# One padded transpose, one joint normalisation and a new order in a three-stage attention and mixture kernel

## The chip, the cores and the metric

The kernel runs on one core of a Trainium2 chip. The metric is the device time of one execution, in microseconds (us). The engines are named as in the profile: PE (matrix products, with PEld for loading the stationary operand), DVE, ACT and POOL (elementwise work), SP (starts the transfers).

## The reference

Three stages follow each other on 4 batches of 448 rows:

```python
scores = (q @ k.T) / 8, masked causally         # 4 batches x 12 heads, 448 x 448, head size 64
attn = exp(scores - max) / sum                  # row by row
x = attn @ v                                    # -> 448 x 768 for each batch
h = relu(x @ w_in)                              # 768 -> 1024
gate = sigmoid(conv over 3 neighbouring rows of h)
x = (h * gate) @ w_out                          # 1024 -> 768
logits = x @ w_gate; the best 2 of 4 experts, softmaxed      # per row
for each expert: q, k, v = x @ wq, wk, wv; out += weight * (causal attention(q, k, v) @ wo)
```

All inputs are float32 in value, the result is 4 x 448 x 768.

## The kernel before, in words

**Attention.** Heads are taken in pairs: 24 pairs in the first stage (6 for each batch) and 8 pairs of experts in the last. `scores` (L625) makes the scores of one pair. The rows of a head lie in four chunks of 64, 128, 128 and 128 rows (c = 0 to 3); chunk c is as wide as the causal mask leaves it, 64, 192, 320 or 448 columns, so a head has four score tiles in two PSUM banks. The first pair of all is computed from the plain inputs (L667). All others are split into a high and a low part, and the products of both heads (three terms for each tile) go to PE as one block of 24 instructions (L676), head 0 in the upper 64 rows of the array and head 1 in the lower 64. DVE then adds the mask and takes the row minimum (L653), ACT takes the exponential with its row sum (L657). For each head DVE adds the row sum and the epsilon (L692) and inverts (L694). After that each of the four chunks of the head is scaled by its reciprocal (L698 on ACT, L701 on DVE or POOL; the experts' coefficient is multiplied in here). The chunks of both heads lie side by side in one tile `e`, 2048 columns wide; the columns from 1920 on hold chunk 0 of both heads, in the upper 64 rows alone.

**Weighing.** `weigh` (L712) turns the scaled weights, 128 x 128 at a time, on PE (L710, through the helper `tr`), 16 turns for a pair. The turn of chunk 0 takes both heads at once: 64 rows with 128 columns become 128 rows with 64 columns, so it uses half of the array's rows; the other 15 take 128 rows. Each four turns fill one PSUM bank, which ACT or DVE copies to SBUF. Then follow the products with v: one over the diagonal chunk (L729, two instructions in the profile) and twelve on half of the array's columns (L735).

**The folded weights.** `w_out` and the experts' projections are multiplied once, at the start, into one matrix (`fold`, L843), from high and low parts (L883), while the first pairs' attention runs.

**The rest.** `products` (L875) issues the three-term products of the hidden layer, the projections and the output, at L883.

**Order.** No loop order reaches the engines as written. Every step is a node with the engines that may take it, an assumed cost for each, and what it reads and writes; a planner (`Plan`, L171) plays the engines through in time and picks the ready node of highest rank. The ranks are then shifted by a list of numbers, `SHIFTS`, over ranges of nodes or of time. All turns have the same assumed cost there, `TURN`, whatever their rows. A dependency within one engine needs no wait; between engines it is a semaphore.

**Filling.** Ten products on zeros (L588) come first on PE, and 30 more (L1085) are placed where the planner finds room.

Of the kernel before, what the change touches and what calls it, by code (L numbers as in the profile page):

```python
# [9 lines left out]
F32 = mybir.dt.float32  # L10
# [3 lines left out]
OP = mybir.AluOpType  # L14
# [21 lines left out]

COL2 = (1920, 1536, 896, 0)
# [5 lines left out]
TURNS = ((0, 4), (4, 6))  # L43
# [7 lines left out]
QUOTA = {"xs": 7, "qks": 4, "y": 4, "vs": 3, "vs2": 2, "w1": 3, "wraw": 1, "ab": 4}  # L51
# [478 lines left out]
def attention_moe_moe(ctx: ExitStack, tc: tile.TileContext, qk, vv, w_in, cw, w_out, wqk, wvg, wo, out):  # L530
# [26 lines left out]
    def tiles(name, n, shape, dtype, pool=None):  # L557
        return [(pool or base).tile(shape, dtype, name=f"{name}{i}") for i in range(n)]

    stats = tiles("stat", 4, [128, 4, 4], F32)  # L560
# [13 lines left out]

    bk = Kind(blocks)
# [13 lines left out]
    for name, kind, quota in (  # L589
            ("xs", pairs, QUOTA["xs"]), ("g", pairs, 8), ("qks", pairs, QUOTA["qks"]), ("wx", pairs, 12),  # L590
            ("y", pairs, QUOTA["y"]), ("q2", pairs, 2), ("k2", pairs, 2),
            ("vs", bk, QUOTA["vs"]), ("gx", gxk, 1), ("vs2", bk, QUOTA["vs2"]), ("w1", slabs, QUOTA["w1"]), ("wraw", half, QUOTA["wraw"]), ("wt", half, 2), ("wxr", half, 2), ("raw", half, 1),
            ("xc", half, 2), ("cv", half, 3), ("o", half, 3), ("gw", half, 1),
            ("hp", Kind(hps), 2), ("st", Kind(stats), 4),
            ("e", Kind(tiles("e", EN, [128, 2048], F32)), EN), ("kb", half, 1), ("ab", half, QUOTA["ab"]),
            ("qw", half, 1),
            ("sx", bank, 2), ("sy", bank, 2),
            ("ta", bank, 1), ("t1", bank, 2), ("tb", bank, 2),
            ("po", bank, PO), ("pf", sums, 2), ("fill", sums, 1)):
        P.tag(name, kind, quota)  # L600
# [21 lines left out]
    NORM = {}  # L622


    def scores(qk, j, e):  # L625
# [8 lines left out]
        sts = [P.buf("st") for _ in range(2)]  # L634
# [12 lines left out]
        def weight(o, c):  # L647

            w, st, sb, rows = Q0[c] + QN[c], sts[o], sbs[o], slice(0, QN[c])

            def mx(_):
                m = mask[rows, 448 - w:448] if c and o else mask[rows, 320:320 + w]
                nc.vector.tensor_tensor_reduce(out=ec(o, c), in0=bank(o, c), in1=m, scale=-0.125, scalar=3.0e38,  # L653
                                               op0=OP.add, op1=OP.min, accum_out=st[rows, 0, c:c + 1])

            def ex(_):
                nc.scalar.activation(ec(o, c), ec(o, c), AF.Exp, bias=st[rows, 0, c:c + 1], scale=-1.0,  # L657
                                     accum_out=st[rows, 1, c:c + 1])

            P.op({"V": on_vector(w)}, mx, r=[(sb[c], c)], w=[(e, (o, c)), (st, ("m", c))])  # L660
            P.op({"A": on_scalar(w) + 0.23}, ex, r=[(st, ("m", c))], w=[(e, (o, c)), (st, ("s", c))])
# [22 lines left out]
        for o, st in enumerate(sts):  # L684
            norms(j + o, st, o, ec, e)

    def norms(j, st, o, ec, e):
        moe = j >= B * H
        b, x = divmod(j - B * H, E)


        P.op({"V": 0.09}, lambda _: nc.vector.tensor_reduce(st[:, 3], st[:, 1:3].rearrange("p a c -> p c a"), axis=AX.X, op=OP.add),  # L692
             r=[(st, ("s", c)) for c in range(4)], w=[(st, "r")])
        P.op({"V": 0.095}, lambda _: nc.vector.reciprocal(st[:, 3], st[:, 3]), w=[(st, "r")])  # L694
        for c in ORDER:
            def norm(en, c=c):
                if en == "A":
                    nc.scalar.activation(ec(o, c), ec(o, c), AF.Copy, scale=st[:QN[c], 3, c:c + 1])  # L698
                else:
                    gate = coef[:QN[c], b, c, x:x + 1] if moe else 1.0  # L700
                    engine(en).tensor_scalar(ec(o, c), ec(o, c), st[:QN[c], 3, c:c + 1], gate, op0=OP.mult, op1=OP.mult)  # L701

            cost = scale_cost(Q0[c] + QN[c])
            if moe:
                cost.pop("A", None)
# [436 lines left out]
```

## Time and profile before

| | us |
|---|---|
| median of 3 runs | 545.47 (545.29 to 546.98) |
| the profiled execution: its own time | 546.95 |
| its span, first to last instruction | 545.2 |
| PE busy | 538.5 (99% of the span) |
| DVE, ACT, POOL busy | 410.1 (75%), 335.2 (61%), 114.7 (21%) |

The engines run beside each other, so the busy times do not add up. A product's row gives the duration of one instruction with its fill and drain (270 ns for a turn), which overlaps with its neighbours; what one costs in a row of them is the distance from its start to the next one's start.

### The profile page before, as it was taken

The page shows a single profiled execution, that of the slowest core. Times are in us where ns is not written, and L with a number is a line of the kernel's source. Part 1 is how long each engine was busy: PE and PEld are TensorE (multiplying, and loading weights), DVE is VectorE, ACT ScalarE, POOL GpSimd, SP SyncE. Part 2 cuts the span into 40 slices and gives each one's busy share as a digit, 9 for nine tenths or more (in the row PEclk, how much of TensorE's full clock was granted, in tenths as well). Part 3 has the DMA queues.
Part 4 walks back from the last instruction along what each step waited for, and adds up shares of the span by engine and source line. Part 5 has one row for each costly group of instructions (what it writes and reads, how often), then busy time and mean ns, then how long its engine had stood idle before and what let it go on. Part 6 is the DMA issues. An engine that isn't in the chain of part 4 may idle for free.

```text
span 545.2 us, 10297 instructions
## 1 busy us (share of the span) xinstructions
PE 538.5 (99%) x3552; PEld 439.6 (81%) x3552; DVE 410.1 (75%) x1273; ACT 335.2 (61%) x951; POOL 114.7 (21%) x132
## 2 busy tenths in 40 slices
PE   8899999999999999999999999999999999999999
PEld 4578896778777897899887777998897778988976
DVE  4997788999998464986477999982368999852761
ACT  2673447779997462763475876873268766641742
POOL 4531013629433020020051332300002102000000
PEclk9899999999999999999999999999999999999999
DMA  8884334666664100546012462670004404620042
GB/s 253 247 217 118 117 135 125 229 198 225 210 228 141 33 3 17 181 167 225 1 52 71 125 199 70 222 253 17 1 35 137 149 4 173 203 87 1 2 159 103
DMA packets 43413, 69.92 MB, mean 128 GB/s; under 512 B 8928, under 2 KB 37344, under 8 KB 43360
## 3 DMA queue, kind: packets, MB, share of 16 engines
q1 hardware_dynamic: 43360, 69.26, 39.4%
q8 instruction: 28, 0.46, 0.3%
q14 instruction: 25, 0.20, 0.1%
HBM read 55.87 MB, written 13.37 MB: 127 GB/s over the span
## 4 chain that ended last, share of the span: by engine, by line
PE 90%; DVE 7%; DMA 2%; issue 1%; ACT 0%; SPq 0%; DVEq 0%; ACTq 0%
PE pf L883 52%; PE bank L710 13%; PE bank L676 9%; PE bank L735 8%; PE bank L729 4%; PE pf L990 1%; DVE work L912 1%; DVE pair L617 1%; DMA work<-in_qk 1%; PE bank L883 1%; DMA work<-in_w_out 1%; DVE e L653 1%; DVE work L804 1%; DVE work L806 1%; PE pf L1085 1%
## 5 line engine op out<-in xcount | busy, mean ns | idle before, releaser
L883 PE MATMUL pf<-pair,slab 128*128 128x448 f32 (+2 forms) x984 | 215.6, 366 | 2.9 <-POOL pair L617 1.2
L883 PEld LDWEIGHTS pf<-pair,slab 128*128 128x128 f32 x984 | 172.2, 189 | 24.1 <-issue 4.6
L657 ACT ACTIVATE e<-e,stat 128x320 f32<-128x320 f32 (+3 forms) x256 | 127.0, 498 | 32.7 <-DVE stat L653 32.1
L653 DVE CUSTOM_DVE_ANT_0 e<-bank,mask 64x64 f32<-64x64 f32 (+3 forms) x256 | 92.5, 413 | 15.0 <-PE bank L676 12.8
L710 PE MATMUL bank<-ident,e 128*128 128x128 f32 (+1 forms) x512 | 84.1, 282 | 0.8 <-ACT hp L901 0.4
L710 PEld LDWEIGHTS bank<-ident,e 128*128 128x128 f32 (+1 forms) x512 | 61.7, 142 | 27.6 <-issue 15.5
L883 PE MATMUL pf<-pair,wqks 128*128 128x448 f32 x384 | 81.8, 369 | 0.0
L883 PEld LDWEIGHTS pf<-pair,wqks 128*128 128x128 f32 x384 | 71.3, 188 | 6.0 <-issue 0.6
L617 POOL TENSOR_TENSOR pair<-work,pair 128x448 fp32r<-128x448 f32 (+1 forms) x36 | 44.6, 1254 | 52.3 <-DVE pair L611 26.3
L611 DVE COPY work<-bank 128x512 f32<-128x512 f32 (+1 forms) x64 | 41.9, 670 | 15.7 <-PE bank L710 13.9
L609 ACT ACTIVATE work<-bank 128x512 f32<-128x512 f32 (+1 forms) x68 | 38.3, 576 | 24.9 <-PE bank L710 21.7
L676 PE MATMUL bank<-pair,pair 64*64 64x64 f32 (+3 forms) x560 | 51.9, 293 | 0.0
L698 ACT ACTIVATE e<-e,stat 128x320 f32<-128x320 f32 (+3 forms) x96 | 42.6, 498 | 11.7 <-DVE stat L694 11.1
L735 PE MATMUL bank<-work,block 128*64 128x128 f32 (+2 forms) x384 | 48.5, 388 | 0.0
L657 ACT ACTIVATION_READ_ACCUMULATOR e<-e,stat 128x1 f32 (+1 forms) x256 | 48.2, 188 | 0.0
L912 DVE SCALAR_TENSOR_TENSOR work<-hp,cws,work 128x448 f32<-128x448 f32 x64 | 44.7, 713 | 2.9 <-ACT work L907 2.3
L617 DVE TENSOR_TENSOR pair<-pf,pair 128x448 fp32r<-128x448 f32 (+3 forms) x32 | 15.4, 501 | 39.6 <-ACT pair L609 39.4
L676 PEld LDWEIGHTS bank<-pair,pair 64*128 64x128 f32 (+1 forms) x560 | 40.0, 173 | 3.4 <-issue 1.5
L613 POOL TENSOR_SCALAR pair<-work 128x896 fp32r<-128x896 f32 (+2 forms) x16 | 17.6, 1101 | 103.8 <-DMA block<-in_vv 57.8
L735 PEld LDWEIGHTS bank<-work,block 128*64 128x64 f32 x384 | 22.5, 136 | 20.7 <-issue 19.2
L883 PE MATMUL pf<-wvs,pair 128*128 128x260 f32 x288 | 37.4, 287 | 0.0
L609 ACT ACTIVATE pair<-pf 128x448 fp32r<-128x448 f32 (+3 forms) x32 | 13.3, 444 | 38.7 <-PE pf L883 37.5
(97 smaller groups left out, 628.0 us busy)
## 6 DMA issues: line engine op xcount, KB each, us to landing
slab<-w_scratch SPq DMA_DIRECT2D x24, 768.0 KB, 4.3
work<-in_w_out SPq DMA_DIRECT2D x8, 768.0 KB, 5.1
work<-in_w_in SPq DMA_DIRECT2D x8, 768.0 KB, 5.7
w_scratch<-slab SPq DMA_DIRECT2D x8, 768.0 KB, 4.4
work<-in_qk SPq DMA_DIRECT2D x24, 224.0 KB, 4.4
out<-work SPq DMA_DIRECT2D x24, 224.0 KB, 2.0
block<-in_vv SPq DMA_DIRECT2D x24, 192.0 KB, 3.3
slab<-wo_scratch SPq DMA_DIRECT2D x6, 768.0 KB, 4.6
```

The lines of the kernel that those rows point to most:

```text
L609: nc.scalar.activation(dst(), src(), AF.Copy)
L611: nc.vector.tensor_copy(dst(), src())
L617: return lambda e: engine(e).tensor_sub(dst(), src(), f32(h()))
L653: nc.vector.tensor_tensor_reduce(out=ec(o, c), in0=bank(o, c), in1=m, scale=-0.125, scalar=3.0e38, op0=OP.add, op1=OP.min, accum_out=st[ro ...
L657: nc.scalar.activation(ec(o, c), ec(o, c), AF.Exp, bias=st[rows, 0, c:c + 1], scale=-1.0, accum_out=st[rows, 1, c:c + 1])
L676: nc.tensor.matmul(bank(o, c), q(s)[own, Q0[c]:Q0[c] + QN[c]], k(t)[own, kc(o, c)], start=i == 0, stop=i == 2)
L698: nc.scalar.activation(ec(o, c), ec(o, c), AF.Copy, scale=st[:QN[c], 3, c:c + 1])
L710: P.op({"T": TURN}, lambda _: nc.tensor.transpose(dst()[:, :n], src()[:n], ident[:n, :n]), r=r, w=keys)
L729: P.op({"T": 4 * S / 2400}, lambda _: nc.tensor.matmul(ps[:, :S], v[:, 0].rearrange("p o d -> p (o d)"), n0[:, :S], start=True, stop=False ...
L735: nc.tensor.matmul(ps[own, Q0[k]:S], v[:, k, o], part(o), start=False, stop=k == 2)
L883: nc.tensor.matmul(out_ap(), a(), b(), start=first, stop=end), r=r, w=[(ps, 0)])
L912: return lambda _: nc.vector.scalar_tensor_tensor(cv[:, :S], hp[:, i:S + i], cws[:, fc, i:i + 1], cv[:, :S], op0=OP.mult, op1=OP.add)
```

## The change

- The turn of chunk 0 takes all 128 rows of `e`. The lower 64 rows of its columns are set to zero once, at the start, by POOL, for each of the three `e` tiles. Its result is 128 columns wide, of which the second 64 fall on the place that chunk 1's turn writes afterwards in the same bank; the extra key `(t, max(c, 1))` makes chunk 1 come after it.
- The row sums of both heads lie in one `stat` tile of twice the size, and one reduction and one reciprocal serve both heads; the scaling of either head waits for them. There are 3 such tiles where there were 4 single ones.
- The scaling steps are listed chunk by chunk with both heads inside, not head by head.
- `SHIFTS` is another list, of 48 entries where there were 64, and the order is planned anew. The quotas and costs of the other steps are the same.

```diff
 SHIFTS = (
-    (22128, 169, 174, 0.25), (15400, 176, 216, 0.5), (27611, 179, 259, 0.5), (50220, 85, 105, 0.5),
...
+    (-1, 2486, 2507, -0.5), (57162, 82, 87, 10), (62964, 276, 356, 1), (63391, 321, 331, 2), (-1, 2573, 2593, -32),
...
-    stats = tiles("stat", 4, [128, 4, 4], F32)
+    stats = tiles("stat", 3, [128, 4, 2, 4], F32)
...
+    weights = tiles("e", EN, [128, 2048], F32)
+    for t in weights:
+        nc.gpsimd.memset(t[HALF[1], COL2[0]:], 0.0)
...
-        P.op({"V": 0.09}, lambda _: nc.vector.tensor_reduce(st[:, 3], st[:, 1:3].rearrange("p a c -> p c a"), axis=AX.X, op=OP.add),
-             r=[(st, ("s", c)) for c in range(4)], w=[(st, "r")])
-        P.op({"V": 0.095}, lambda _: nc.vector.reciprocal(st[:, 3], st[:, 3]), w=[(st, "r")])
+        P.op({"V": 0.1}, lambda _: nc.vector.tensor_reduce(st[:, 3].rearrange("p o c -> p (o c)"), st[:, 1:3].rearrange("p a o c -> p (o c) a"), axis=AX.X, op=OP.add),
+             r=[(st, ("s", o, c)) for o in range(2) for c in range(4)], w=[(st, "r")])
+        P.op({"V": 0.11}, lambda _: nc.vector.reciprocal(st[:, 3], st[:, 3]), w=[(st, "r")])
         for c in ORDER:
-            def norm(en, c=c):
...
+            for o in range(2):
+                def norm(en, c=c, o=o):
...
-    def tr(dst, src, r, keys, n=128):
+    def tr(dst, src, r, keys):
 
-        P.op({"T": TURN}, lambda _: nc.tensor.transpose(dst()[:, :n], src()[:n], ident[:n, :n]), r=r, w=keys)
+        P.op({"T": TURN}, lambda _: nc.tensor.transpose(dst(), src(), ident[:, :]), r=r, w=keys)
...
-               [(e, (o, c)) for o in range(2)], [(t, c)], QN[c])
+               [(e, (o, c)) for o in range(2)], [(t, c), (t, max(c, 1))])
```

PE, in the hidden layer of the second batch, before: L883 are its products, L710 the turns (the row with 128x64 is chunk 0's), `e` the weights of a pair.

```order
1131 L883 MATMUL pf_141<-pair_134,slab_137 128x448
1132 L883 MATMUL pf_142<-pair_120,slab_137 128x448
1133 L883 MATMUL pf_142<-pair_120,slab_138 128x448
1134 L710 MATMUL bank_145<-ident,e_159 128x64
1135 L710 MATMUL bank_145<-ident,e_159 128x128 x3
1136 L710 MATMUL bank_144<-ident,e_159 128x128 x2
1137 L883 MATMUL pf_142<-pair_120,slab_137 128x448
```

The same engine and layer in the change, where the lines have the numbers L877, L704 and, for the products on half of the columns, L729:

```order
1093 L729 MATMUL bank_151<-work_143,block_97 64x128 x2
1094 L729 MATMUL bank_151<-work_143,block_97 64x256 x2
1095 L704 MATMUL bank_146<-ident,e_113 128x128 x4
1096 L877 MATMUL pf_145<-pair_126,slab_140 128x448
1097 L877 MATMUL pf_145<-pair_126,slab_141 128x448
1098 L704 MATMUL bank_150<-ident,e_113 128x128 x4
1099 L877 MATMUL pf_145<-pair_126,slab_140 128x448
```

The single row of 128x64 is gone; chunk 0 is one of the four turns of full size.

DVE, at the end of a pair's exponentials in the first stage, before: L692 is the reduction, L694 the reciprocal, L701 a scaling, `stat` one head's sums.

```order
238 L617 TENSOR_TENSOR pair_121<-bank_145,pair_121 128x448
239 L692 TENSOR_REDUCE stat_84<-stat_84 128x4
240 L694 RECIPROCAL stat_84<-stat_84 128x4
241 L701 TENSOR_SCALAR e_161<-e_161,stat_84 128x320
242 L701 TENSOR_SCALAR e_161<-e_161,stat_84 128x448
243 L692 TENSOR_REDUCE stat_85<-stat_85 128x4
244 L694 RECIPROCAL stat_85<-stat_85 128x4
```

DVE at such a place in the change (L685, L687, L695; L608 are copies):

```order
226 L608 COPY work_143<-bank_151 128x512
227 L614 TENSOR_TENSOR wvs<-pf_145,wvs 128x260
228 L685 TENSOR_REDUCE stat_84<-stat_84 128x8
229 L687 RECIPROCAL stat_84<-stat_84 128x8
230 L695 TENSOR_SCALAR e_115<-e_115,stat_84 128x320
231 L695 TENSOR_SCALAR e_115<-e_115,stat_84 64x64
```

Two reductions and two reciprocals became one of each, and all scalings of the pair stand behind them.

PE after the first filling products, before: L883 with 512 or 260 columns are the folded weights, L667 the scores of the first pair.

```order
56 L883 MATMUL pf_141<-pair_120,slab_137 128x512
57 L883 MATMUL pf_142<-pair_120,slab_137 128x260
58 L667 MATMUL bank_145<-work_140 64x64
59 L667 MATMUL bank_146<-work_140 128x320
60 L667 MATMUL bank_146<-work_140 128x192
61 L883 MATMUL pf_141<-pair_120,slab_137 128x512
62 L883 MATMUL pf_141<-pair_121,slab_137 128x512
63 L667 MATMUL bank_145<-work_140 128x448
```

The same place in the change (L661 are the first pair's scores, L1079 filling products, L877 the folded weights):

```order
53 L661 MATMUL bank_151<-work_143 128x192
54 L661 MATMUL bank_148<-work_143 128x192
55 L661 MATMUL bank_149<-work_143 64x64
...
60 L661 MATMUL bank_150<-work_143 64x64
...
65 L877 MATMUL pf_144<-pair_121,slab_140 128x512
66 L877 MATMUL pf_145<-pair_121,slab_140 128x260
67 L877 MATMUL pf_144<-pair_121,slab_140 128x512
68 L877 MATMUL pf_144<-pair_122,slab_140 128x512
```

All eight score products of the first pair now stand ahead of the first folded product, and the second pair's scores follow its first ten.

## Rows read from the trace of the kernel before

**Rows 1.** Page, part 1: busy us (share of span) and instructions by engine.
```profile
PE 538.5 (99%) x3552; PEld 439.6 (81%) x3552; DVE 410.1 (75%) x1273; ACT 335.2 (61%) x951; POOL 114.7 (21%) x132
```
**Rows 2.** Windows: stretch, its us, each engine's busy us, PEclk, DMA share, GB/s.
```profile
17.50:23.50 6.00, 3.67 (x19) 2.38 (x17) 5.93 (x15) 4.27 (x13) 4.62 (x5) 1.00 0.81 254
23.50:27.00 3.50, 3.29 (x14) 2.72 (x14) 2.41 (x5) 2.11 (x5) 1.17 (x1) 0.55 0.99 278
40.00:200.00 160.00, 158.82 (x1089) 130.23 (x1088) 136.44 (x392) 112.49 (x319) 56.16 (x49) 1.00 0.47 152
200.00:400.00 200.00, 200.00 (x1333) 168.59 (x1333) 144.41 (x458) 118.31 (x338) 29.23 (x36) 1.00 0.33 109
400.00:537.00 137.00, 137.00 (x922) 112.25 (x921) 97.43 (x333) 78.81 (x232) 11.47 (x15) 1.00 0.28 95
```
**Rows 3.** Waits of PE: line, for whom, total us, times, longest.
```profile
PE pf L588 <- DVE tri L549: 1.7, 1, 1.7
PE pf L883 <- POOL pair L617: 1.2, 1, 1.2
PE pf L883 <- DVE pair L617: 1.0, 1, 1.0
PE pf L883 <- ACT hp L901: 0.7, 1, 0.7
PE bank L710 <- ACT hp L901: 0.4, 1, 0.4
PE bank L710 <- ACT e L698: 0.2, 1, 0.2
```
**Rows 4.** Timeline of PE near 212 us: start us, us to the last one's end, instructions.
```profile
212.09 0.49 PE L710 MATMUL bank<-ident,e 128*128 128x128 f32 x3
```
**Rows 5.** Timeline of PE, 211 to 217 us: turns of chunk 0 between others.
```profile
211.30 0.39 PE L735 MATMUL bank<-work,block 128*64 128x256 f32 x2
211.62 0.27 PE L710 MATMUL bank<-ident,e 64*128 64x64 f32 x1
211.82 0.44 PE L710 MATMUL bank<-ident,e 128*128 128x128 f32 x2
...
215.70 0.49 PE L710 MATMUL bank<-ident,e 128*128 128x128 f32 x3
216.12 0.27 PE L710 MATMUL bank<-ident,e 64*128 64x64 f32 x1
216.32 0.54 PE L735 MATMUL bank<-work,block 128*64 128x384 f32 x1
```
**Rows 6.** Groups by shape: line, engine, tile of the array, count, busy us, mean ns, idle before.
```profile
L710 PE MATMUL bank<-ident,e 128*128 128x128 f32 x480 | 78.7, 282 | 0.8 <-ACT hp L901 0.4 <-ACT e L698 0.2
L710 PE MATMUL bank<-ident,e 64*128 64x64 f32 x32 | 8.8, 275 | 0.0
L710 PEld LDWEIGHTS bank<-ident,e 64*128 64x128 f32 x32 | 4.4, 137 | 6.8 <-issue 5.4 <-DVE stat L653 0.9
```
**Rows 7.** Timeline of PE, 17 to 24 us.
```profile
17.99 0.49 PE L710 MATMUL bank<-ident,work 128*128 128x128 f32 x3
19.67 1.32 PE L883 MATMUL pf<-pair,slab 128*128 128x512 f32 x6 [1.19 <-POOL pair L617]
20.82 1.15 PE L710 MATMUL bank<-ident,e 128*128 128x128 f32 x4
23.00 0.62 PE L883 MATMUL pf<-pair,slab 128*128 128x512 f32 x2 [1.02 <-DVE pair L617]
```
**Rows 8.** Groups by shape on DVE, ACT and POOL that the change touches.
```profile
L694 DVE RECIPROCAL stat<-stat 128x4 f32<-128x4 f32 x64 | 10.4, 171 | 1.1
L692 DVE TENSOR_REDUCE stat<-stat 128x4 f32<-128x8 f32 x64 | 9.3, 151 | 2.6 <-ACT e L657 2.4
L657 ACT ACTIVATE e<-e,stat 128x192 f32<-128x192 f32 x64 | 28.4, 445 | 11.5 <-DVE stat L653 11.4
L657 ACT ACTIVATION_READ_ACCUMULATOR e<-e,stat 128x1 f32 x192 | 36.1, 188 | 0.0
```
**Rows 9.** Timeline of POOL, 3 to 12 us.
```profile
2.99 1.24 POOL L572 MEMSET block<- 64x64 f32 x7
4.17 0.97 POOL L771 MEMSET work<- 64x448 f32 x2
10.57 1.83 POOL L617 TENSOR_TENSOR pair<-work,pair 128x772 fp32r<-128x772 f32 x1 [5.43 <-ACT pair L609]
```
**Rows 10.** Timeline of PE, first folded product and first scores.
```profile
10.49 0.62 PE L883 MATMUL pf<-pair,slab 128*128 128x512 f32 x2
11.04 1.23 PE L667 MATMUL bank<-work 128*64 128x64 f32 x5
```
**Rows 11.** Timeline of DVE: reductions of the two heads of two pairs.
```profile
400.49 0.15 DVE L692 TENSOR_REDUCE stat<-stat 128x4 f32<-128x8 f32 x1
400.76 0.15 DVE L692 TENSOR_REDUCE stat<-stat 128x4 f32<-128x8 f32 x1
...
421.51 0.15 DVE L692 TENSOR_REDUCE stat<-stat 128x4 f32<-128x8 f32 x1
424.18 0.15 DVE L692 TENSOR_REDUCE stat<-stat 128x4 f32<-128x8 f32 x1
```

More of the change, by code (lines that the diff above doesn't have):

```diff
@@ L34 @@
 HALF = (slice(0, 64), slice(64, 128))
+TURNS = ((0, 4), (4, 6))
 COL2 = (1920, 1536, 896, 0)
@@ L42 @@
 TILES = (((0, 1, 1), (0, 2, 1), (0, 3, 1), (0, 3, 3)), ((1, 1, 1), (1, 2, 1), (1, 3, 1), (1, 3, 3)), ((0, 2, 2), (0, 3, 2), (1, 2, 2), (1, 3, 2)))
-TURNS = ((0, 4), (4, 6))
 SWITCH = 0.2
@@ L50 @@
 PAIRS, VALUES, UNITS, SLABS, EN, PO = 18, 6, 15, 3, 3, 1
-QUOTA = {"xs": 7, "qks": 4, "y": 4, "vs": 3, "vs2": 2, "w1": 3, "wraw": 1, "ab": 4}
+QUOTA = {"xs": 7, "qks": 4, "y": 4, "vs": 3, "vs2": 2, "w1": 3, "wraw": 1, "ab": 4, "qw": 1, "kb": 1, "raw": 1}
 WARM = 10
@@ L591, in attention_moe_moe @@
             ("y", pairs, QUOTA["y"]), ("q2", pairs, 2), ("k2", pairs, 2),
-            ("vs", bk, QUOTA["vs"]), ("gx", gxk, 1), ("vs2", bk, QUOTA["vs2"]), ("w1", slabs, QUOTA["w1"]), ("wraw", half, QUOTA["wraw"]), ("wt", half, 2), ("wxr", half, 2), ("raw", half, 1),
+            ("vs", bk, QUOTA["vs"]), ("gx", gxk, 1), ("vs2", bk, QUOTA["vs2"]), ("w1", slabs, QUOTA["w1"]), ("wraw", half, QUOTA["wraw"]), ("wt", half, 2), ("wxr", half, 2), ("raw", half, QUOTA["raw"]),
             ("xc", half, 2), ("cv", half, 3), ("o", half, 3), ("gw", half, 1),
-            ("hp", Kind(hps), 2), ("st", Kind(stats), 4),
-            ("e", Kind(tiles("e", EN, [128, 2048], F32)), EN), ("kb", half, 1), ("ab", half, QUOTA["ab"]),
-            ("qw", half, 1),
+            ("hp", Kind(hps), 2), ("st", Kind(stats), 3),
+            ("e", Kind(weights), EN), ("kb", half, QUOTA["kb"]), ("ab", half, QUOTA["ab"]),
+            ("qw", half, QUOTA["qw"]),
             ("sx", bank, 2), ("sy", bank, 2),
@@ L620, in load @@
         return lambda e: nc.sync.dma_start(dst(), src)
-    NORM = {}
     def scores(qk, j, e):
@@ L633, in scores @@
             sb[0], sb[1] = sb[3], sb[2]
-        sts = [P.buf("st") for _ in range(2)]
+        st = P.buf("st")
         def bank(o, c):
@@ L647, in weight @@
         def weight(o, c):
-            w, st, sb, rows = Q0[c] + QN[c], sts[o], sbs[o], slice(0, QN[c])
+            w, sb, rows = Q0[c] + QN[c], sbs[o], slice(0, QN[c])
             def mx(_):
@@ L653, in mx @@
                 nc.vector.tensor_tensor_reduce(out=ec(o, c), in0=bank(o, c), in1=m, scale=-0.125, scalar=3.0e38,
-                                               op0=OP.add, op1=OP.min, accum_out=st[rows, 0, c:c + 1])
+                                               op0=OP.add, op1=OP.min, accum_out=st[rows, 0, o, c:c + 1])
             def ex(_):
[L657 to L661, printed above, removed]
+                nc.scalar.activation(ec(o, c), ec(o, c), AF.Exp, bias=st[rows, 0, o, c:c + 1], scale=-1.0,
+                                     accum_out=st[rows, 1, o, c:c + 1])
+            P.op({"V": on_vector(w)}, mx, r=[(sb[c], c)], w=[(e, (o, c)), (st, ("m", o, c))])
+            P.op({"A": on_scalar(w) + 0.23}, ex, r=[(st, ("m", o, c))], w=[(e, (o, c)), (st, ("s", o, c))])
         if whole:
@@ L682, in scores, with norms @@
                     weight(o, c)
-        for o, st in enumerate(sts):
-            norms(j + o, st, o, ec, e)
-    def norms(j, st, o, ec, e):
+        norms(j, st, ec, e)
+    def norms(j, st, ec, e):
         moe = j >= B * H
         b, x = divmod(j - B * H, E)
-        P.op({"V": 0.09}, lambda _: nc.vector.tensor_reduce(st[:, 3], st[:, 1:3].rearrange("p a c -> p c a"), axis=AX.X, op=OP.add),
-             r=[(st, ("s", c)) for c in range(4)], w=[(st, "r")])
-        P.op({"V": 0.095}, lambda _: nc.vector.reciprocal(st[:, 3], st[:, 3]), w=[(st, "r")])
+        P.op({"V": 0.1}, lambda _: nc.vector.tensor_reduce(st[:, 3].rearrange("p o c -> p (o c)"), st[:, 1:3].rearrange("p a o c -> p (o c) a"), axis=AX.X, op=OP.add),
+             r=[(st, ("s", o, c)) for o in range(2) for c in range(4)], w=[(st, "r")])
+        P.op({"V": 0.11}, lambda _: nc.vector.reciprocal(st[:, 3], st[:, 3]), w=[(st, "r")])
@@ L695, in norms @@
         for c in ORDER:
-            def norm(en, c=c):
[L697 to L705, printed above, removed]
@@ L706, in norms @@
-            NORM[j] = P.op(cost, norm, r=[(st, "r")] + ([(COEF, b)] if moe else []), w=[(e, (o, c))])
-    def tr(dst, src, r, keys, n=128):
-        P.op({"T": TURN}, lambda _: nc.tensor.transpose(dst()[:, :n], src()[:n], ident[:n, :n]), r=r, w=keys)
+            for o in range(2):
+                def norm(en, c=c, o=o):
+                    if en == "A":
+                        nc.scalar.activation(ec(o, c), ec(o, c), AF.Copy, scale=st[:QN[c], 3, o, c:c + 1])
+                    else:
+                        gate = coef[:QN[c], b, c, x + o:x + o + 1] if moe else 1.0
+                        engine(en).tensor_scalar(ec(o, c), ec(o, c), st[:QN[c], 3, o, c:c + 1], gate, op0=OP.mult, op1=OP.mult)
+                cost = scale_cost(Q0[c] + QN[c])
+                if moe:
+                    cost.pop("A", None)
+                P.op(cost, norm, r=[(st, "r")] + ([(COEF, b)] if moe else []), w=[(e, (o, c))])
```

24 rows, old and new, of the table SHIFTS are left out of this document.

## The prediction

> **What bounds the kernel now.** I read the busy times first, then the table of stretches, then the waits of PE, then the single steps of PE. PE is busy for 538.5 of 545.2 us, while DVE stands at 75% and ACT at 61% [rows 1]. In the stretches from 200 to 400 us and from 400 to 537 us PE is busy for the whole stretch; from 40 to 200 us it misses 1.2 us of 160 [rows 2]. The named waits of PE add up to about 5 us, and four of the six lines are single events [rows 3]. So PE sets the end, and a change counts by what it does to the steps of PE. A busy PE is not PE at its peak, though, and the steps themselves have to be looked at. In a row of turns of 128 rows, three take 0.49 us, of which the last one's own 0.27 overlaps: (0.49 - 0.27) / 2 = 0.11 us from start to start [rows 4]. The 64-row turn breaks this: the 128-row turn ahead of it starts at 215.92 (the third of the three from 215.70, at 0.11 each) and it starts at 216.12, 0.20 later; the one that starts at 211.62 is followed by a 128-row turn at 211.82, again 0.20 later [rows 5]. PE counts as busy in this time, because durations overlap; it shows on the loading of the stationary operand, which is idle for 6.8 us ahead of these 32 turns, 5.4 of it without a releaser [rows 6].
>
> The Trainium skill has a rule for it: "TensorEngine Tiling (Array Packing)", section Key Properties, says that a change of the tiling mode drains TensorE. It also has one that speaks against the change: "TensorE: Matmul & The Clock Gate", section Why this matters for your kernels, says that a single product over 32 rows takes the time of one over 128, so by it nothing is won by the rows. The steps of 0.20 agree with the first [rows 5].
>
> **The change part by part.**
>
> *The full turn.* A 64-row turn between 128-row work costs a longer step into it and a longer step out of it, each 0.20 - 0.11 = 0.09 us too long [rows 4, 5]. This holds where the neighbour uses the whole array. Behind a product on half of the columns the step is 0.31 (211.31 to 211.62) [rows 5], and it is the same 0.31 when a 128-row turn follows there, since the tile changes either way; there nothing is won. I counted the neighbours on PE in both orders. Of the 32 turns of chunk 0, 28 come behind work on the whole array and 29 stand ahead of such work: 57 changes of tile that go. In all PE changes its tile 266 times in the old order (two instructions for a float32 product counted as two) and 209 times in the new one; the difference is exactly these 57, so the new order neither adds nor saves others. 57 x 0.09 = 5.1 us. The wider result of the full turn is in this sum already: in and out together cost twice 0.20 before and twice 0.11 after. Bounds: with each step read 0.01 us too high or too low, 4.6 to 5.7.
>
> *The zeros.* Three memsets of 64 x 128 on POOL at the start. The nearest rows: 64 x 64 takes 0.15 us (7 in 1.24 us, with what follows) and two of 64 x 448 take 0.97 [rows 9]. So they cost between 3 x 0.15 and 3 x 0.49 us; POOL ends its memsets at 5.14 and is idle for 5.43 us until 10.57 [rows 9]. Behind them in POOL's queue stand the two memsets of the first pair's keys; these would end by 6.6 at the latest, and the first scores start after 11 us [rows 10]. Cost 0; without that idle time up to 1.5.
>
> *One reduction, one reciprocal.* 64 x 0.151 + 64 x 0.171 = 20 us of DVE [rows 8] become half as many, each on twice as many elements (8 out of 16, instead of 4 out of 8): between the same duration, if it is all fixed cost, and twice it: DVE saves 0 to 10 us. DVE is not what PE waits for: of PE's waits only 1.0 us is named on DVE in the body [rows 3]. On PE's time I take 0, bounds 0 to -1.0.
> The price is a wait: head 0's scalings now need head 1's sums. Before, the second reduction came 0.27 us (400.49 to 400.76) to 2.67 us (421.51 to 424.18) behind the first [rows 11]. Behind the joint reduction DVE has the eight scalings, and behind these on PE come the turns. But the turn of chunk 0 needs both heads in either version, and while a pair's weights wait, PE has products of the other stage: its wait for scalings is 0.2 us in the whole run [rows 3]. I take 0 here; the other end is a rival below.
>
> *The extra key.* Chunk 1's turn has to follow chunk 0's in the same bank. Both are on PE, in order: no wait. The copy of the bank waited for all four anyway.
>
> *The new order.* All of it is new, and in the body I take what it does beyond the tile changes as 0: the old one leaves no more than 1.2 us of PE idle between 40 and 200 us, and nothing after that [rows 2], so there is little to win, and a worse one would have to show new waits. The start is another matter. Between 17.5 and 23.5 us PE is busy for 3.67 us of 6.0, 2.3 idle [rows 2], because the folded products wait for POOL and DVE to split the weights (1.19 and 1.02 us) [rows 7]. Behind it the granted clock falls to 0.55 of full, its lower level 1.2 GHz for most of the 3.5 us [rows 2]; at full clock that work would take about 1.6 us less. So 2.3 + 1.6 = 3.9 us are lost there. In the new order all eight score products of the first pair come ahead of the first folded one, which then starts some 4 us later than the 10.49 of before [rows 10], and the second pair's scores follow after ten. POOL and DVE thus have more time to split weights before PE asks for them; on the other hand DVE's maxima of all eight tiles now come in among these splits. Bounds: 3.9 gained, or, if the clock falls once more and for as long, 3.9 lost. I take 1.2 gained, a third of what there is, since the folded products start later, but DVE also comes to their low parts later.
>
> Sum on the profiled execution (546.95, span 545.2 and 1.75 around it): 546.95 - 5.1 - 1.2 = 540.65. That execution was the slowest of the three; against the median of 545.47 the same 6.3 us give 539.2.
>
> **The rivals.**
>
> *A, the start gives all back.* No wait and no lower clock in the first 30 us: 545.47 - 5.1 - 3.9 = 536.5. For it: the order there was changed most. Against it: the amount of splitting is the same, and DVE is busy for 5.93 of 6.00 us there [rows 2].
>
> *B, hidden anyway.* PE comes earlier to each join and waits there for ACT or DVE by what it saved: 545.5. For it: ACT and DVE reach 136.4 and 112.5 us in the 160 between 40 and 200 us [rows 2]. Against it: after 200 us PE has no idle time at all and DVE and ACT stand at 72 and 59% (144.4 and 118.3 of 200) [rows 2]; it takes 5 us of new waits.
>
> *C, the padding costs.* The 0.20 us is not the change of tile but a cost of every turn behind another bank or semaphore, and stays. Then twice the columns cost: 128 instead of 64 columns at 0.11 for 128 is 0.055 more, times 32 is 1.8 us: 547.3. Against it: the same 128-row instruction takes 0.11 among its like [rows 4], and the excess appears in the two steps around the 64-row turn only [rows 5].
>
> *D, slower: the joint normalisation shows on PE.* The first head's turns come later by one exponential and its accumulator read, 0.445 + 0.188 = 0.63 us [rows 8], at each pair in which PE has nothing else ready. With 16 of the 32 pairs that is 10.1 us: 545.47 - 6.3 + 10.1 = 549.3. It decides from about 10 pairs on, where 6.3 us eat up the gain. For it: the pair in rows 11 whose heads lie 2.67 us apart. Against it: the wait of 0.2 us named above.
>
> **How the numbers follow.** The forecast, 539.2, has a chance of 0.72; A 0.15; B 0.05; C 0.03; D 0.05. A measurement of this kernel can tell about 0.3%, 1.6 us, from no change. Faster by more than that: the forecast and A, 0.87. Within: B, 0.05. Slower: C (1.8 us) and D, 0.08. The range reaches down to 535.5, which is A with the 1.0 us that DVE's bound allows, and up to 543.0, where the start loses 2.6 us of its 3.9 (545.47 - 5.1 + 2.6). B, C and D lie outside.
>
> **What would show it.** Right: the groups by shape have no turn on 64*128, 512 turns of `e` on 128*128 in their place, and the idle time ahead of their loading falls by about 5 us; starts of four turns in a row are 0.11 apart with chunk 0 among them; PE is still busy for whole stretches after 200 us, with a span of 537 to 540. The start: between 10 and 30 us PE's idle time and the stretch below full clock are together less than 3.9 us. Wrong: a full turn of chunk 0 still 0.20 from its neighbours (C); waits of PE for L692's and L698's successors in the list, of some us, after 100 us (B, D); a longer stretch at the lower clock (the start's other end).

## The result and the profile after

The changed kernel takes 540.73 us in the median of four executions (540.62 to 541.83), against 545.70 (545.29 to 546.98) for the kernel before beside it: a ratio of 0.991, with a 95% interval of 0.9888 to 0.9931. That is 5.0 us faster. The profiled executions lie 6.3 us apart, 546.95 and 540.68 (spans of 545.2 and 538.9); why they differ by more is told below.

The first part of the page of the kernel after: busy us, share of the span and instructions of each engine.
```profile
PE 530.6 (98%) x3550; PEld 437.5 (81%) x3552; DVE 413.1 (77%) x1224; ACT 331.7 (62%) x947; POOL 97.5 (18%) x122
```
PE still sets the end. Its busy time fell by 7.9 us against [rows 1], while its idle time (span less busy) rose from 6.7 to 8.3 us. DVE has 49 instructions fewer and is none the less busier.

The table of stretches of the kernel after: stretch, its us, busy us of PE, PEld, DVE, ACT and POOL, granted clock, DMA share, GB/s.
```profile
17.50:23.50 6.00, 5.63 (x50) 4.83 (x50) 4.95 (x18) 5.55 (x13) 5.49 (x4) 1.00 0.66 183
23.50:27.00 3.50, 3.50 (x36) 2.71 (x34) 3.45 (x12) 3.50 (x15) 1.28 (x2) 1.00 1.09 368
27.00:40.00 13.00, 11.72 (x73) 9.19 (x70) 12.96 (x36) 9.01 (x29) 4.92 (x6) 1.00 0.81 235
40.00:200.00 160.00, 157.03 (x1062) 130.85 (x1061) 133.55 (x342) 103.18 (x285) 42.20 (x38) 1.00 0.48 147
200.00:400.00 200.00, 200.00 (x1370) 168.67 (x1369) 155.31 (x490) 128.56 (x378) 30.02 (x41) 1.00 0.36 114
```
Against [rows 2], PE's first gap has gone (3.67 to 5.63 us of 6.0) and the clock stays at full speed. But a new gap of 1.3 us stands between 27 and 40 us, and between 40 and 200 us PE now misses 3.0 us instead of 1.2. How much of these differences belongs to the order is worked out below.

The waits of PE in the kernel after: line, for whom, total us, times, longest us.
```profile
PE bank L704 <- DVE e L695: 1.8, 2, 1.1
PE pf L585 <- DVE tri L543: 1.7, 1, 1.7
PE bank L704 <- DVE stat L647: 0.9, 2, 0.5
PE pf L877 <- DVE wqks L614: 0.8, 1, 0.8
PE pf L877 <- DVE slab L614: 0.7, 1, 0.7
```
The head of the list is new. In [rows 3] the turns (now L704) waited 0.2 us for scalings; now they wait 1.8 us for scalings on DVE, in two events.

The groups by shape that answer to [rows 6] and [rows 8], of the kernel after: line, engine, operation, tile, count, busy us, mean ns of one, idle before.
```profile
L704 PE MATMUL bank<-ident,e 128*128 128x128 f32 x512 | 74.8, 276 | 2.7 <-DVE e L695 1.8 <-ACT e L692 0.4 <-DVE stat L647 0.4
L704 PEld LDWEIGHTS bank<-ident,e 128*128 128x128 f32 x512 | 59.3, 140 | 21.2 <-issue 7.6 <-DVE e L695 3.0 <-DVE stat L647 2.5
...
L687 DVE RECIPROCAL stat<-stat 128x8 f32<-128x8 f32 x32 | 6.4, 201 | 0.9
L685 DVE TENSOR_REDUCE stat<-stat 128x8 f32<-128x16 f32 x32 | 5.2, 161 | 5.6 <-ACT e L651 5.4
```
The group on 64*128 is gone, and 512 turns of 128 rows stand in its place. Reductions and reciprocals fell from 19.7 to 11.6 us of DVE.

PE's timeline where the weights of several pairs are turned in a row, of the kernel after: start us, us to the last one's end, instructions.
```profile
208.83 1.53 PE L704 MATMUL bank<-ident,e 128*128 128x128 f32 x12
```
Twelve turns in 1.53 us, chunk 0's among them: (1.53 - 0.27) / 11 = 0.115 us from start to start. The 0.20 of [rows 5] has gone.

### The profile page after: what moved, and what is told of

Its sections match the earlier page's. It is cut to its first block, busy times and chain, and to the rows that moved or that the text cites. A ratio compares the mean times of both kernels' runs of the same rounds, so it can differ in the third digit from the quotient of the medians.

```text
span 538.9 us, 10192 instructions
## 1 busy us (share of the span) xinstructions
PE 530.6 (98%) x3550; PEld 437.5 (81%) x3552; DVE 413.1 (77%) x1224; ACT 331.7 (62%) x947; POOL 97.5 (18%) x122
## 4 chain that ended last, share of the span: by engine, by line
PE 69%; DVE 3%; ACT 2%; DMA 1%; issue 0%; DVEq 0%; ACTq 0%
PE pf L877 41%; PE bank L704 8%; PE bank L670 7%; PE bank L729 6%; PE bank L723 4%; PE pf L984 1%; DVE work L906 1%; DMA work<-in_w_in 1%; PE bank L877 1%; ACT e L651 1%; PE pf L1079 1%; DVE work L914 0%; ACT e L692 0%; DVE work L798 0%; DVE work L800 0%; ACT pair L606 0%
## 5 line engine op out<-in xcount | busy, mean ns | idle before, releaser
L877 PE MATMUL pf<-pair,slab 128*128 128x448 f32 (+2 forms) x984 | 215.7, 367 | 1.6 <-DVE wqks L614 0.8
L877 PEld LDWEIGHTS pf<-pair,slab 128*128 128x128 f32 x984 | 171.8, 188 | 23.7 <-issue 6.1
L651 ACT ACTIVATE e<-e,stat 128x320 f32<-128x320 f32 (+3 forms) x256 | 126.8, 498 | 24.0 <-DVE stat L647 23.7
L647 DVE CUSTOM_DVE_ANT_0 e<-bank,mask 128x320 f32<-128x320 f32 (+3 forms) x256 | 92.7, 414 | 5.4 <-PE bank L670 4.9
L877 PE MATMUL pf<-pair,wqks 128*128 128x448 f32 x384 | 81.6, 369 | 0.5 <-ACT pair L606 0.5
L704 PE MATMUL bank<-ident,e 128*128 128x128 f32 x512 | 74.8, 276 | 2.7 <-DVE e L695 1.8
L877 PEld LDWEIGHTS pf<-pair,wqks 128*128 128x128 f32 x384 | 71.4, 188 | 7.1 <-ACT pair L606 0.9
L704 PEld LDWEIGHTS bank<-ident,e 128*128 128x128 f32 x512 | 59.3, 140 | 21.2 <-issue 7.6
L608 DVE COPY work<-bank 128x512 f32<-128x512 f32 (+1 forms) x63 | 40.6, 666 | 25.1 <-PE bank L704 22.1
L614 POOL TENSOR_TENSOR pair<-work,pair 128x448 fp32r<-128x448 f32 (+1 forms) x35 | 43.5, 1256 | 53.5 <-ACT pair L606 25.4
L729 PE MATMUL bank<-work,block 128*64 128x128 f32 (+2 forms) x384 | 48.5, 388 | 0.0
L729 PEld LDWEIGHTS bank<-work,block 128*64 128x64 f32 x384 | 22.5, 136 | 23.9 <-issue 21.1
L692 ACT ACTIVATE e<-e,stat 128x448 f32<-128x448 f32 (+3 forms) x88 | 39.0, 508 | 3.6 <-DVE stat L687 3.4
L877 PE MATMUL pf<-wvs,pair 128*128 128x260 f32 x288 | 37.7, 286 | 0.0
L877 PEld LDWEIGHTS pf<-wvs,pair 128*128 128x128 f32 x288 | 35.3, 188 | 1.2 <-issue 0.6
```

What stands on the lines that cost most here:

```text
L608: nc.vector.tensor_copy(dst(), src())
L614: return lambda e: engine(e).tensor_sub(dst(), src(), f32(h()))
L704: P.op({"T": TURN}, lambda _: nc.tensor.transpose(dst(), src(), ident[:, :]), r=r, w=keys)
L729: nc.tensor.matmul(ps[own, Q0[k]:S], v[:, k, o], part(o), start=False, stop=k == 2)
L877: nc.tensor.matmul(out_ap(), a(), b(), start=first, stop=end), r=r, w=[(ps, 0)])
```

## The experiments

Two questions stood. First: do the vanished tile changes carry the gain (theory T), or the new order and the joint normalisation? Second: why does PE now wait for scalings? Theory P says that scalings on DVE stand still while POOL works, and that PE pays for it. Beside each run the kernel before ran on the same chip, with medians of 545.5 us.

**Chunk 0 over 64 rows again, in the new order** (266 tile changes, all else as after):
```
-    def tr(dst, src, r, keys):
+    def tr(dst, src, r, keys, n=128):
-        ... nc.tensor.transpose(dst(), src(), ident[:, :]) ...
+        ... nc.tensor.transpose(dst()[:, :n], src()[:n], ident[:n, :n]) ...
```


> The changed kernel, in its own order instruction by instruction, with chunk 0 turned over 64 rows again; the zeros, the joint reduction and the new order stay. PE changes its tile 266 times instead of 209. Theory T (the gain is the 57 changes of tile at 0.09 us): 540.7 + 5.1 = 545.8 us, the same as the kernel before. Rival O (the gain is the new order, above all its start): stays at 540.7. Rival N (the gain is the joint reduction on DVE): stays at 540.7.

Measured: 546.85 us, ratio 1.002 (1.001 to 1.0031). Against the kernel after that is 6.1 us, or 0.107 for each of 57 changes, and 1.0 more than T expected. So the tile changes carry the gain, and rivals O and N have fallen. Something else shows: with the same number of changes, the new order and the joint normalisation are together 1.3 us slower than the old kernel.

**The full turn alone, in the old order** (the copied bank is left as it was, so in part of the pairs the zeros overwrite 64 columns; the work is the same):
```
+    weights = tiles("e", EN, [128, 2048], F32)
+    for t in weights:
+        nc.gpsimd.memset(t[HALF[1], COL2[0]:], 0.0)
-        ... nc.tensor.transpose(dst()[:, :n], src()[:n], ident[:n, :n]) ...
+        ... nc.tensor.transpose(dst(), src(), ident[:, :]) ...
```


> The kernel before, in its own order, with the zeros and the turn of chunk 0 over all 128 rows; nothing else is changed. In 17 of the 32 pairs chunk 1 is turned before chunk 0 there, and half of its result is overwritten with zeros, so this kernel only tells the time. 209 changes of tile instead of 266. Theory T: 545.7 - 5.1 = 540.6 us, the whole gain without the new order. Rivals O and N: 545.7, or 547.5 if the wider result costs 0.055 us for each turn.

Measured: 540.05 us, ratio 0.9899 (0.9879 to 0.9918). The whole gain is there without the new order: 5.5 us, or 0.096 a change. Two of its five executions took 541.6 us, at a lower granted clock, of which more below.

**Two reductions and two reciprocals again, in the new order:**
```
+ [nc.vector.tensor_reduce(st[:, 3, o], st[:, 1:3, o].rearrange("p a c -> p c a"), ...) for o in range(2)]
+ [nc.vector.reciprocal(st[:, 3, o], st[:, 3, o]) for o in range(2)]
```


> The changed kernel with the joint reduction and the joint reciprocal issued as two each, one for each head, at the same place in the same order; the scalings still wait for both. DVE gets 32 x (0.16 + 0.20) = 10 to 11 us of work back. Theory T: PE does not wait for DVE there, 540.7 us, at most 541.7. Rival N: 545.7 if the gain came from this.

Measured: 541.36 us, ratio 0.9913 (0.9896 to 0.993). That is 0.6 above the kernel after with widely overlapping intervals, so no effect of the joint instructions on the time can be told. The dose was smaller than the 10 to 11 us expected. The page of this run:
```profile
PE 530.2 (98%) x3550; PEld 437.3 (81%) x3552; DVE 415.0 (77%) x1288; ACT 331.7 (62%) x947; POOL 97.8 (18%) x122
```
DVE is busy for 1.9 us more than in the kernel after, with 64 instructions more. Part of the reason is that two that follow each other overlap: the two groups are busy for 15.6 us against 11.6, where single durations add up to more. The two heads are still scaled behind both sums here, so this run tells nothing of that wait.

**The kernel before once more, unchanged:**

> The kernel before, unchanged, for a second profile. In the first profile TensorE's granted clock fell to half between 23.5 and 27.0 us, and that execution took 546.95 where the median is 545.5. If the fall belongs to the order (two waits of PE for split weights), it is there again, and the changed kernel's start wins its 1.6 us in every execution. If it came by chance, this profile has none, about 545.4 us, and the time before and after differs by the changes of tile alone.

Measured: 545.42 us, ratio 0.9995 (0.9984 to 1.0006). Its profile answers the question of the clock. The stretches of this run of the same program, columns as above:
```profile
17.50:23.50 6.00, 3.77 (x20) 2.45 (x18) 5.93 (x15) 4.37 (x13) 4.61 (x5) 1.00 0.86 271
23.50:27.00 3.50, 3.25 (x23) 1.99 (x24) 3.47 (x6) 3.02 (x7) 1.01 (x1) 1.00 0.92 250
27.00:40.00 13.00, 13.00 (x91) 10.76 (x90) 12.01 (x38) 9.70 (x28) 5.85 (x5) 1.00 0.88 246
40.00:200.00 160.00, 158.77 (x1089) 130.28 (x1088) 137.31 (x395) 113.03 (x321) 55.02 (x48) 1.00 0.46 148
```
The gap from 17.5 to 23.5 us is nearly the same as in [rows 2] (2.2 us against 2.3), yet the clock behind it is 1.00 instead of 0.55. So the lower clock came with some executions, not with every one; this one has a span of 544.0 us against 545.2. In the profile of the kernel with the full turn alone it fell to 0.59 in that stretch. The two executions of the kernel before are one program with one order.

The executions on record say how often it comes. Of 57 executions of the kernel before beside these runs, 10 show a mean granted clock of 0.997 instead of 1.000; these ten took 546.6 to 547.7 us, and the others 545.0 to 545.9. With the full turn in the old order it is 2 of 10. Of 46 executions of the kernel after and of its variants, which keep its order, none shows it. So the fall goes with the old order, in about one execution of six: there the new start wins some 1.5 us, and a median doesn't show it. What decides within the old order is not shown.

**Two scalings moved from DVE to ScalarE** (of the kernel after, the two for which PE waits):
```
+SCALED, ON_SCALAR = [], (14, 18)
+                    if en == "V":
+                        SCALED.append(0)
+                        if len(SCALED) - 1 in ON_SCALAR:
+                            en = "A"
```
The three timelines on which it rests are of the kernel after. DVE's first, in two stretches:
```profile
99.23 0.39 DVE L695 TENSOR_SCALAR e<-e,stat 128x320 f32<-128x320 f32 x1
...
99.53 3.02 DVE L695 TENSOR_SCALAR e<-e,stat 64x64 f32<-64x64 f32 x1
...
119.79 1.92 DVE L695 TENSOR_SCALAR e<-e,stat 128x192 f32<-128x192 f32 x1
```
POOL's:
```profile
99.37 0.93 POOL L695 TENSOR_SCALAR e<-e,stat 64x64 f32<-64x64 f32 x2
100.28 2.23 POOL L614 TENSOR_TENSOR pair<-work,pair 128x448 fp32r<-128x448 f32 x2
...
119.77 1.82 POOL L614 TENSOR_TENSOR slab<-work,slab 128x768 fp32r<-128x768 f32 x1
```
PE's:
```profile
103.37 0.87 PE L704 MATMUL bank<-ident,e 128*128 128x128 f32 x6 [1.08 <-DVE e L695]
...
121.77 0.66 PE L704 MATMUL bank<-ident,e 128*128 128x128 f32 x4 [0.68 <-DVE e L695]
```
The smallest scaling there is, 64x64, takes 3.02 us instead of some 0.24. It starts within POOL's row of 99.37, and ends at 102.55, just behind POOL's last at 102.51. The one of 119.79 ends at 121.71, behind POOL's 121.59. PE's turns come next, 1.08 and 0.68 us late.

> The changed kernel in its own order; two scalings of weights in the first hidden layer, that DVE took 3.02 us (64 x 64, at 99.5 us) and 1.92 us (128 x 192, at 119.8 us) for while POOL was at work, go to ACT at the same place of the order. Theory P (the changed kernel loses what its start wins because DVE stands still during POOL's instructions and PE then waits for these scalings, 1.24 and 0.84 us): the first wait goes, the second shrinks, 539.2 to 539.8 us, and DVE has no instruction at L695 over 1.3 us after 90 us. Rival Q (the turns would have waited for something else, the new order is late there anyway): 540.7.

Measured: 538.83 us, ratio 0.9873 (0.9856 to 0.989), and 539.13, 0.9876 (0.9855 to 0.9897), when it ran again with others later. So 1.6 to 1.9 us came back, as P has it, and a little more than expected. The intervals of both still touch that of the kernel after (0.9888 to 0.9931); what settles it is that the two waits went, and the run with five scalings below. One point of the expectation failed: a long scaling on DVE is still there. DVE's timeline with the two moved:
```profile
100.74 0.62 DVE L609 COPY work<-bank 128x448 f32<-128x448 f32 x1 [0.33 <-PE bank L709]
101.28 2.14 DVE L700 TENSOR_SCALAR e<-e,stat 128x192 f32<-128x192 f32 x1
```
and PE's behind it:
```profile
103.48 0.77 PE L709 MATMUL bank<-ident,e 128*128 128x128 f32 x5 [0.43 <-DVE e L700]
```
The next scaling in DVE's queue (now L700) ran into the same pair of instructions on POOL, which here lasts until 103.30, and PE's wait for it is 0.4 us. The copy ahead of it reads a PSUM bank and keeps its usual time beside POOL.

What this second run expected:

> The kernel with two scalings on ACT once more, beside the one with five: 538.8 us.

**Five scalings moved to ScalarE** (the same edit, with 1, 14, 15, 18 and 21):

> As the kernel with two scalings on ACT, and three more that DVE met POOL in: 128 x 448 at 38.6 us (1.19 us), 128 x 192 at 101.3 us (2.14 us there, 0.30 before) and 128 x 448 at 163.4 us (1.17 us). Theory P: PE still waits 0.59 us at 102.6 and 0.47 at 160.8 us; with the first gone and the rest unclear, 538.0 to 538.5 us. Rival Q: these scalings are not what PE waits for, 538.8.

Measured: 537.84 us (537.16 to 538.08), ratio 0.9856 (0.9841 to 0.9871), the fastest of all, and better than expected. Its waits of PE and its stretch from 40 to 200 us:
```profile
PE pf L586 <- DVE tri L544: 1.7, 1, 1.7
PE pf L882 <- DVE slab L615: 1.1, 1, 1.1
PE pf L882 <- DVE wqks L615: 0.8, 1, 0.8
PE bank L709 <- DVE stat L648: 0.7, 2, 0.4
PE pf L882 <- ACT pair L607: 0.5, 1, 0.5
```
```profile
40.00:200.00 160.00, 159.41 (x1090) 133.25 (x1089) 130.20 (x349) 107.71 (x302) 43.88 (x39) 1.00 0.48 148
```
No wait for a scaling is left, and PE misses 0.6 us instead of 3.0. These 2.4 us are most of the 2.9 between the medians of this kernel and the one after, and here the intervals lie apart.

**The full turn in the old order, made whole:** chunk 0's turn goes to the last 128 columns of the bank, where its zeros meet nothing, and the copy is issued as two.
```
-   tr(lambda c=c, t=t: t[:, Q0[c]:Q0[c] + 128], ...
+   tr(lambda t=t, m=Q0[c] - 64 if c else 384: t[:, m:m + 128], ...
+   first = [high(lambda: n0[:, 64:S], lambda t=t: t[:, :384]), high(lambda: n0[:, :64], lambda t=t: t[:, 384:448])]
```


> The kernel before in its own order with the zeros and the full turn of chunk 0, made whole: chunk 0's result goes to the last 128 columns of its bank, so that it touches no other chunk's, and the copy of the bank is issued as two instructions (384 and 64 columns). Neither the joint reduction nor the new order. ACT or DVE get one more instruction of 0.2 us for each pair, 6 us in all, off PE's path. Theory T: as without the second copy, 540.1 us, 0.6 faster than the changed kernel. Rival (the copies stand between PE's turns and its products, and each pair waits 0.2 us more): up to 546.

Measured: 540.14 us (539.82 to 540.28), ratio 0.9896 (0.988 to 0.9913). The old order with the full turn does at least as well as the kernel after (the 0.6 us between them are within the intervals); the second copy costs nothing that shows.

**The price of a turn and of a change, by addition.** To the kernel after, one more turn of chunk 0 is added ahead of the full one, writing the same columns. In one kernel it has 128 rows (no new change of tile), in the other 64 (57 new ones):
```
+            if twice:
+                nc.tensor.transpose(dst(), src(), ident[:, :])                     # in the one
+                nc.tensor.transpose(dst()[:, :64], src()[:64], ident[:64, :64])    # in the other
             nc.tensor.transpose(dst(), src(), ident[:, :])
```


> The changed kernel in its own order, with the full turn of chunk 0 issued twice: 32 more turns over 128 rows among their like, no change of tile. Price of a plain turn, 0.11 us: 540.7 + 3.5 = 544.2 us.

> The changed kernel in its own order, with a 64-row turn of chunk 0 ahead of the full one: as many more turns as 32, of half the size, and 57 more changes of tile. Theory T (a step of 0.20 into the tile and one of 0.20 out of it, instead of one of 0.11): 32 x 0.29 = 9.3, less where the neighbour changes the tile anyway: 540.7 + 8.7 = 549.4 us. If the time belonged to the turn's size: 540.7 + 1.8 = 542.5.

Measured: 544.78 us for 128 rows, ratio 0.9982 (0.9972 to 0.9992), and 550.56 for 64 rows, 1.0089 (1.0072 to 1.0107). The added full turn costs (544.78 - 540.73) / 32 = 0.127 us, a little more than its step. The added turn of half the rows costs (550.56 - 540.73) / 32 = 0.31. Per change of tile that is (550.56 - 544.78) / 57 = 0.10 us. PE's timeline shows it step by step, the added turn in the middle; with 128 rows first:
```profile
207.86 0.27 PE L707 MATMUL bank<-ident,e 128*128 128x128 f32 x1
207.97 0.27 PE L706 MATMUL bank<-ident,e 128*128 128x128 f32 x1
208.08 0.38 PE L707 MATMUL bank<-ident,e 128*128 128x128 f32 x2
```
and with 64:
```profile
210.38 0.27 PE L707 MATMUL bank<-ident,e 128*128 128x128 f32 x1
210.59 0.27 PE L706 MATMUL bank<-ident,e 64*128 64x64 f32 x1
210.79 0.44 PE L707 MATMUL bank<-ident,e 128*128 128x128 f32 x2
```
Starts 0.11 apart in the one, 0.21 and 0.20 in the other. A third step is longer too: the two turns of the last row take 0.38 us in the one and 0.44 in the other, of which the second one's own 0.27 overlaps, so their starts are 0.11 and 0.17 apart. A single turn lasts 0.27 us in either kernel: the duration hides the price, the starts show it.

## Why the prediction was right, and where it was not

**The full turn: right in mechanism, a little small in size.** Forecast: 5.1 us, bounds 4.6 to 5.7. Measured: 5.5 us in the old order, 6.1 in the new one, 5.8 by addition, so 0.096 to 0.107 a change. The forecast left out the third step. In [rows 5] the two turns that start at 211.82, behind a turn of 64 rows, take 0.44 us, and two among their like take 0.38: the step between them is 0.17 instead of 0.11. In the trace of the kernel before, 23 of the 32 turns of chunk 0 have two such turns behind them. Four of the 23 stand behind work on half of the columns, where the longer step stays; 19 times 0.06 is 1.1 us more (an estimate from these rows), 6.2 together. PE's busy time at full clock bears it out: from 536.9 us in the second profile of the kernel before it fell by 6.3 to 530.5 (full turn in the old order, made whole) and 530.6 (the kernel after), and from 537.4 (64-row turn in the new order) by 6.8. Waits took some of it back.

The idle time ahead of the turns' loading was to fall by about 5 us. To the 6.8 us of [rows 6] for chunk 0 belong those of the other 480 turns before:
```profile
L710 PEld LDWEIGHTS bank<-ident,e 128*128 128x128 f32 x480 | 57.3, 142 | 20.8 <-issue 10.1 <-DVE stat L653 1.5 <-ACT e L698 1.5
```
and with the full turn alone:
```profile
L713 PEld LDWEIGHTS bank<-ident,e 128*128 128x128 f32 x512 | 60.9, 142 | 21.6 <-issue 10.1 <-DVE stat L656 1.9 <-ACT e L701 1.5
```
So it fell from 27.6 to 21.6 us, and the part without a releaser from 15.5 (10.1 and 5.4) to 10.1, as forecast. In the kernel after it is 21.2 and 7.6: the further fall of the latter came with the new order, where 3.0 us for late scalings came in.

**Rival C has fallen; B came in a small part.** A full turn steps at 0.11 beside its like, as the timelines at 208 us show. But some of the time saved was given back at a join. The full turn in the old order, made whole, its stretch from 40 to 200 us and its largest wait there:
```profile
40.00:200.00 160.00, 157.96 (x1099) 131.08 (x1098) 136.86 (x396) 113.56 (x330) 48.93 (x48) 1.00 0.46 148
PE pf L887 <- ACT hp L905: 1.5, 1, 1.5
```
PE misses 2.0 us there instead of 1.2, and waits 1.5 us for `hp` instead of 0.7 [rows 3].

**The joint instructions: no effect on PE, as forecast.** The two groups on DVE fell by 8.1 us, within the bounds of 0 to 10, though DVE as a whole was busy for 3.0 us more. The lower bound of -1.0 on PE's time took a wait of the start, 1.02 us at 23.00 [rows 7], for one of the body. (Two other readings enter no sum: all six waits of [rows 3] are single events, not four, and the old list of `SHIFTS` has 75 entries, not 64.)

**The start: right in sign, smaller in size, and counted on a base that was not typical.** The forecast was 1.2 gained of 3.9. What it was to show holds: from 10 to 30 us PE is idle for 1.04 us, without a lower clock. But the sign could not tell the kernels apart: the kernel before meets it too in its second profile, with 2.48 us. The stretches, of after:
```profile
10.00:30.00 20.00, 18.96 (x134) 13.66 (x133) 18.83 (x55) 16.20 (x47) 9.03 (x7) 1.00 0.82 250
0.00:40.00 40.00, 35.91 (x213) 24.68 (x214) 33.33 (x104) 26.29 (x75) 18.04 (x37) 1.00 0.83 243
```
and of the kernel before in its second profile:
```profile
10.00:30.00 20.00, 17.52 (x100) 11.83 (x99) 17.78 (x44) 13.56 (x33) 11.68 (x10) 1.00 0.84 243
0.00:40.00 40.00, 35.55 (x193) 23.51 (x194) 31.47 (x93) 23.11 (x58) 19.36 (x34) 1.00 0.87 251
```
In these executions at full clock 1.4 us of idle time go between 10 and 30 us, but the new gap behind 27 us takes most of it back: 0.4 remains over 40 us. More than half of that gap is a wait of PE for DVE:
```profile
33.31 6.55 PE L877 MATMUL pf<-pair,slab 128*128 128x512 f32 x36 [0.76 <-DVE wqks L614]
32.58 0.68 DVE L614 TENSOR_TENSOR wqks<-pf,wqks 128x512 fp32r<-128x512 f32 x1
```
By the names in these rows it is another wait than those of [rows 7]: the products read `pair` and `slab`, not `wqks`, and write `pf`, which DVE's instruction reads until 33.26. So PE waits there until a bank of finished products has been read out, and not for split weights. The 1.6 us for the lower clock came with the one profiled execution, and with about one in six, and is not in the median of 545.5. Taking a gain from it over to the median was wrong: it explains most of why the profiled executions lie 6.3 us apart and the medians 5.0. For the same reason rival A, 536.5, could not come: 1.6 of its 3.9 us were not in the median to be given back.

**The step that failed: "the new order ... in the body I take what it does beyond the tile changes as 0".** It costs. PE's idle time from 40 to 200 us rose from 1.2 to 3.0 us. The full turn alone raised it to 2.0 (above), and the new order with turns of 64 rows to 2.4:
```profile
40.00:200.00 160.00, 157.58 (x1052) 129.41 (x1051) 132.27 (x334) 101.60 (x280) 41.93 (x38) 1.00 0.48 147
```
The old order's waits for `hp` [rows 3] have gone and others have come: 1.76 of the 3.0 us are the two waits behind scalings that stood still beside POOL. Moving scalings off DVE gave 1.6 to 1.9 us for two and 2.9 for five. Over the whole run, new order and joint normalisation together cost 1.3 us with the 64-row turn (546.85 against 545.5, an interval of 0.1 to 0.3% above the kernel before); with the full turn, the 0.7 us (540.73 against 540.05) are within the intervals. The prediction asked for "new waits" as the sign of it, and for some us of them after 100 us as a sign of being wrong: the two, 1.8 us, end at 103.4 and 121.8. Rival D looked at the right place, turns that wait for scalings; but its mechanism, the first head behind the second's sums, had no price of 10 us, and what showed is another one.

The Trainium skill has it: "SBUF — State Buffer", section SBUF: two separate sides, says that GpSimd (POOL) shares one pair of ports with those VectorE (DVE) instructions that run in a two-port mode, or read two inputs from SBUF while GpSimd reads it, and that whoever starts first holds the pair for its whole instruction while the other blocks. The trace of the kernel after agrees in that all nine of the 84 scalings in the row below that took over 1.3 times the median of their shape lay beside an instruction on POOL. No run here shows the mode they ran in or what decides, since twelve others lay beside one too and kept their time. And the trace shows more, since the scaling of 3.02 us lay beside four instructions on POOL in a row and ended behind the last. The view of one tile gives a group's shortest, median and longest duration in ns, and is where such a thing shows. The scalings on DVE in the kernel before:
```profile
L701 DVE TENSOR_SCALAR e<-e,stat x67: 231/381/1421, 23.3 to 440.4; 128x320 f32<-128x320 f32 x20, 64x64 f32<-64x64 f32 x17, 128x448 f32<-128x448 f32 x17, 128x192 f32<-128x192 f32 x13
```
and in the kernel after:
```profile
L695 DVE TENSOR_SCALAR e<-e,stat x84: 235/372/3024, 38.0 to 435.3; 128x192 f32<-128x192 f32 x24, 128x320 f32<-128x320 f32 x22, 64x64 f32<-64x64 f32 x21, 128x448 f32<-128x448 f32 x17
```
The longest of 1.4 us before, at a median of 0.38, was a warning that the prediction did not read. Standing still is in fact not new: by the same measure eleven of the 67 before were long, in sum 6.0 us over their medians, and nine of the 84 after, 7.9 us. New is that PE waits for two of them; before, it waited for none on DVE.

In sum: 5.5 to 6.1 from the tile changes, 0.7 to 1.3 given back, 5.0 measured, where 5.1 and 1.2 had been added to 6.3. The forecast of 539.2 was 1.5 low, inside its range. The largest term was too small and the two others were too good, so that the sum came this near is partly luck.

**Not settled:** whether it is the list that sets the order or the wait for both heads' sums that leaves PE with nothing ahead of these scalings. The old order with the joint instructions was not tried.

## What to carry to other kernels

Look at start-to-start steps of small matmuls and turns, not at durations: a single one on another part of the array pays on its way in and out, and on the step behind, and zeros that let it use the same tile as its neighbours can be cheaper than fewer rows. Before a new order is taken as free, look at the longest duration of each group, not the mean: one instruction of 3 us among 84 with a median of 0.37 cost PE a microsecond here, once PE had to wait for it. And profile the kernel before twice: what differs between two executions of it is not in the median, and does not belong into a forecast of the median.

## What the runs showed of the hardware beyond what was expected

- A change of the array's tile cost 0.096 to 0.107 us in three pairs of kernels, taken over the whole run. Around a 64-row turn among turns of 128 rows three steps are longer, 0.20, 0.20 and 0.17 us instead of 0.11.
- A scaling on DVE, float32 from SBUF to SBUF, took from 0.24 to 3.02 us. In the kernels before and after all long ones lay beside an instruction on POOL, and the two that PE waited for ended 0.04 and 0.12 us behind it; a copy from a PSUM bank took its usual 0.62 us beside the same work.
- The granted clock fell to 0.55 and 0.59 behind the gap at 17.5 us in two profiles with the old order, and stayed at 1.00 behind nearly the same gap in two others (3.77 and 3.64 us busy of 6.0). In times, it fell in 12 of 67 executions with the old order and in none of 46 with the new one.
